# A fused attention, expert and feed-forward kernel: attention cut into one-engine jobs that the kernel's own list scheduler orders and pins

## The chip, the cores and the metric

The kernel runs on one core of a Trainium2 chip. The metric is the device time of one launch in microseconds (us). Before the change three launches took 1038.58, 1032.4 and 1031.0 us; their median is 1032.4 us.

## The reference

Three stages run one after the other, all in float32. B=4 batches, H=8 heads, S=768 steps and D=48 make 32 independent recurrences; the token rows are 3072 by 384.

```python
# 1. attention (delta rule), for every b, h; k_n = k / (|k| + 1e-6), state starts at 0
for t in range(S):
    y[t] = q[t] @ state
    state += beta[t] * outer(k_n[t], v[t] - k_n[t] @ state)
x = y.transpose(0, 2, 1, 3).reshape(B * S, H * D)
# 2. experts, top-1 of E=8, F=1024
logits = x @ w_gate + modality_bias[modality_id]
e = argmax(logits);  g = softmax(logits)[e]
x = g * (relu(x @ w1[e]) @ w2[e])
# 3. feed-forward, 2048 wide
h = x @ w_in
out = (h * sigmoid(h)) @ w_out
```

## The kernel before, in words

**Attention.** The 768 steps are cut into six tiles t of 128 steps, each with two halves e of 64 steps; the 32 recurrences (b, h) are two groups p of two batches, 16 recurrences each. For one (t, p) the work is a chain of small products on TensorE (PE), each group of which writes one of five PSUM banks that ScalarE (ACT) or VectorE (DVE) empties:

- `grams`: four groups `gr` of 8 products k·k and k·q (L158). ACT copies k·k to G (L161). The k·q part goes to KB with its upper triangle cleared, in one of two ways that `mask` names: DVE multiplies by a mask while it copies (L166, "v"), or ACT copies (L173, "p") and GpSimd (POOL) clears afterwards (L181). Then ACT moves a 32-wide diagonal block inside G (L177).
- `lanes`: DVE transposes the diagonal blocks of both p into L, one recurrence's block to a lane (L230); ACT takes roots for the norms (L197); DVE scales, multiplies v by the lengths (`lengthen`, L213), and inverts all unit triangular 32-blocks in 31 dependent steps (L237, L249, L259, L267). `spread` transposes the inverses back into G (L275), and `spread_upper` transposes them again, the other way round, into T (L284), whose halves two DMAs move to other partitions (L288). `gather` copies the blocks into KA (L293, by ACT or by DMA).
- `merge`: PE joins the blocks (px L308, then po L320 from X and T), and forms weights (pw L335, L338), which ACT negates into KA.
- `rec`: for each half e PE computes the update pu (L365), the next state ps (L376) and the read py (L388), 32 small products each; ACT copies them to Z (L369, L380) and Y (L396). The 16 products of each of the two batches lie in the two column halves of PE's array. `zip="zss"` says that pu takes the two halves in turn, and ps and py first all of one, then all of the other.
- Y goes to HBM and is transposed (xt L608), six products give the router's logits (pl L621 and L627), and DVE adds the bias (lg L629). This last line is called gate(t) here. The lanes of t+1 depend only on the grams of t+1; the recurrence of t+1 needs the lanes of t+1 and the state of t.

**Experts.** `Router.rank` and `finish` (the "wave") turn logits into slots: group 0 (tiles 0 to 2) into five slots of 256 tokens, group 1 (tiles 3 to 5) into four of 512. Weights are split into a high and a low part (ACT L950, DVE L951); a slot gathers its tokens, runs ph (L991) and poe (L1002) in 8 pieces, and scatters. The slots of group 0 can start when tile 2 is ranked, and so lie beside the attention of the later tiles; group 1 must wait for gate(5).

**Feed-forward.** Six groups of 512 tokens: fph (L1232), silu, fpo (L1249).

**What sets the order.** In `run` every step of attention gets a position from hand-set numbers (S, F, L, G, A, M, R, D, W, Z of PLAN), and the steps are written in order of position. Tile, the framework, then schedules the instructions of all stages onto the five in-order engines; `Experts.regular` is written after attention and fills in between.

Of the kernel before, what the change touches and what calls it, by code (L numbers as in the profile page):

```python
# [34 lines left out]

class Attention:
    B, H, S, D = 4, 8, 768, 48

    def __init__(self, tc, ident, pools, kq, qb, kd, vd, beta, xs):
# [30 lines left out]


        self.G = cp.tile([128, 4, N, 64], F32, name="G")
        self.st = [{} for _ in range(T)]
        self.todo = [[], []]

    NB = 6

    def copier(self, x):

        nc = self.nc  # L80
        return {"a": nc.scalar.copy, "v": nc.vector.tensor_copy, "p": nc.gpsimd.tensor_copy, "d": nc.sync.dma_start}[x]
# [18 lines left out]


    def setup_early(self):
# [8 lines left out]
    def betas(self):  # L111
        self.nc.sync.dma_start(self.bl, self.beta)

    def setup_late(self):
        nc = self.nc
        for z in self.KI:
            for e, r in enumerate((slice(64, 128), slice(0, 64))):
                c = slice(64 * (1 - e), 64 * (1 - e) + 48)
                nc.scalar.copy(z[r, e], self.ident[r, None, c].to_broadcast([64, self.U // 2, 48]))
        for z in self.KA:  # L120
            nc.gpsimd.memset(z, 0.0)
        nc.gpsimd.memset(self.Z[0][64:128], 0.0)
        nc.gpsimd.memset(self.Z[1][0:64], 0.0)


    def fetch(self, t, p):
        for i in range(2):
            self.nc.sync.dma_start(self.keys(t, p, i).rearrange("p u m c -> p (u m c)"), self.kq[t, p, i])

    def fetch_more(self, t, p):  # L130
        nc, KB = self.nc, self.kb(t, p)
        for e in range(2):
            r = slice(64 - 64 * e, 128 - 64 * e)
            nc.sync.dma_start(KB[r, e], self.qb[t, p, r])
        vs = self.st[t]["vs", p] = self.pools["ld"].tile(
            [128, self.U // 2, self.D], F32, tag="kr", name=f"vs{t}_{p}", bufs=4
        )
        nc.sync.dma_start(vs, self.vd[t, p])

    def fetch_late(self, t, p):  # L140
# [4 lines left out]


    def grams(self, t, ps):
# [37 lines left out]

        return [lambda p=p, i=i: step(p, i) for p in ps for i in range(n)]


    def scales(self, t):


# [1262 lines left out]
```

## Time and profile before

| what | value |
|---|---|
| three launches | 1031.0, 1032.4, 1038.58 us (median 1032.4) |
| profiled execution | 1032.07 us, of which 1030.3 us are the span of the trace |
| granted TensorE clock, mean | 0.925 of full speed |
| busy in the span | PE 903.2 us (88%), DVE 595.7 (58%), ACT 484.3 (47%), POOL 103.9 (10%) |
| gate(5), the end of attention | bias added at 384.12 us |

The span falls into two parts. Up to gate(5) attention runs, with the experts of the first three tiles filled in. After it come the experts of the other tiles and the feed-forward. Busy time counts the time in which an engine executes something; the granted clock is the share of its full speed that the chip gave TensorE in that stretch.

### The profile page before, as it was taken

How to read it: one execution, taken by the hardware profiler on the slowest of the kernel's cores; microseconds unless marked ns; L12 is line 12 of the kernel's file. 1: busy time of each engine (PE TensorE's matmuls, PEld its weight loads, DVE VectorE, ACT ScalarE, POOL GpSimd, SP SyncE). 2: the span in 40 equal slices, each digit the busy share in tenths (PEclk: the TensorE clock that was granted, in tenths of full speed). 3: DMA queues.
4: the chain of work that ended last, by engine and by line, in shares of the span. 5: the costliest groups of instructions: out<-in, count | busy, mean ns of one | idle time of the engine just before them, and what ended most of it. 6: DMA issues, size and time to landing. Idle time of an engine off the chain costs nothing. (4 is left out here: it accounts for less than half of the span.)

```text
span 1030.3 us, 22690 instructions
## 1 busy us (share of the span) xinstructions
PE 903.2 (88%) x9126; PEld 818.9 (79%) x9126; DVE 595.7 (58%) x1714; ACT 484.3 (47%) x980; POOL 103.9 (10%) x100
## 2 busy tenths in 40 slices
PE   5266867684879998989999899999999999999998
PEld 5255757674768887988898799999899999999997
DVE  4996939577673337999997337553333333333333
ACT  5435555565646765646665445433333233332322
POOL 5100000000120010142341101000000000000000
PEclk7657979597889998999999999999999999999999
DMA  8943636160353144146676132200100000000000
GB/s 224 275 143 68 174 79 183 38 156 17 84 171 69 41 118 157 39 137 213 219 229 191 62 99 63 78 31 0 32 31 31 1 31 1 31 1 1 31 1 31
DMA packets 65253, 92.29 MB, mean 90 GB/s; under 512 B 25225, under 2 KB 49943, under 8 KB 65136
## 3 DMA queue, kind: packets, MB, share of 16 engines
q1 hardware_dynamic: 61808, 80.90, 27.3%
q0 software_dynamic: 3328, 9.83, 2.9%
q8 instruction: 73, 1.20, 0.5%
q14 instruction: 44, 0.36, 0.1%
HBM read 79.18 MB, written 14.55 MB: 91 GB/s over the span
## 5 line engine op out<-in xcount | busy, mean ns | idle before, releaser
L1249 PE MATMUL fpo<-o,fgh 128*128 128x384 f32 x768 | 184.3, 338 | 0.0
L1237 DVE TENSOR_TENSOR fy<-fph,fy 128x512 f32<-128x512 f32 x96 | 66.4, 692 | 161.5 <-ACT fy L1235 161.0
L1249 PEld LDWEIGHTS fpo<-o,fgh 128*128 128x128 f32 x768 | 139.3, 188 | 7.9 <-ACT fgh L1239 0.4
L1235 ACT ACTIVATE fy<-fph 128x512 f32<-128x512 f32 x96 | 57.5, 599 | 169.0 <-PE fph L1232 166.1
L1249 PE MATMUL fpo<-o,fgl 128*128 128x384 f32 x384 | 116.6, 338 | 0.0
L1232 PE MATMUL fph<-fxh,ih 128*128 128x512 f32 x288 | 113.7, 395 | 0.0
L1232 PE MATMUL fph<-fxl,ih 128*128 128x512 f32 x288 | 113.3, 394 | 0.0
L1232 PE MATMUL fph<-fxh,il 128*128 128x512 f32 x288 | 113.2, 393 | 0.0
L1241 DVE TENSOR_TENSOR fgl<-fy,fgh 128x512 fp32r<-128x512 f32 x96 | 66.5, 692 | 74.7 <-ACT fgh L1239 64.3
L1239 ACT CAST fgh<-fy 128x512 fp32r<-128x512 f32 x96 | 59.7, 622 | 80.6 <-DVE fy L1237 44.6
L1002 PE MATMUL poe<-wKT,pairs 128*128 128x384 f32 x384 | 75.9, 343 | 3.2 <-ACTq L1093 3.2
L1002 PEld LDWEIGHTS poe<-wKT,pairs 128*128 128x128 f32 x384 | 68.6, 191 | 6.4 <-ACTq L1093 3.5
L259 DVE TENSOR_TENSOR tmp<-A,L 128x126 f32<-128x126 f32 (+20 forms) x336 | 72.3, 252 | 0.4
L267 DVE TENSOR_TENSOR A<-A,tmp 128x126 f32<-128x126 f32 (+20 forms) x336 | 72.3, 252 | 0.2
L1249 PEld LDWEIGHTS fpo<-o,fgl 128*128 128x128 f32 x384 | 71.1, 188 | 0.5
L951 DVE TENSOR_TENSOR wRH<-raw,wRH 128x384 fp32r<-128x384 f32 x72 | 39.5, 554 | 54.3 <-ACT wRH L950 43.1
L1232 PEld LDWEIGHTS fph<-fxl,ih 128*128 128x128 f32 x288 | 54.1, 188 | 10.5
L1232 PEld LDWEIGHTS fph<-fxh,il 128*128 128x128 f32 x288 | 54.1, 188 | 9.6
L1232 PEld LDWEIGHTS fph<-fxh,ih 128*128 128x128 f32 x288 | 54.1, 188 | 9.0
L991 PE MATMUL ph<-xhl,wRH 128*128 128x256 f32 x360 | 57.6, 305 | 3.3 <-DVE wRH L951 1.5
L950 ACT CAST wRH<-raw 128x384 fp32r<-128x384 f32 x72 | 36.8, 514 | 46.3 <-PE ph L991 37.4
L376 PE MATMUL ps<-Z,KI 128*48 128x48 f32 x704 | 43.2, 229 | 16.7 <-ACT Z L369 14.4
(418 smaller groups left out, 1688.6 us busy)
## 6 DMA issues: line engine op xcount, KB each, us to landing
raw<-in_moe_w_dram SPq DMA_DIRECT2D x72, 384.0 KB
KKQ<-in_kq_dram SPq DMA_DIRECT2D x16, 512.0 KB
KB<-in_qb_dram SPq DMA_DIRECT2D x24, 256.0 KB
ri<-in_moe_w_in_dram SPq DMA_DIRECT2D x12, 512.0 KB
ro<-in_moe_w_out_dram SPq DMA_DIRECT2D x16, 384.0 KB
vs<-in_vd_dram SPq DMA_DIRECT2D x12, 384.0 KB
KI<-in_kd_dram SPq DMA_DIRECT2D x24, 192.0 KB
Z<-vs SPq DMA_DIRECT2D x24, 192.0 KB
```

Of the source, the lines that this page charges most:

```text
L259: nc.vector.tensor_tensor(tv, r[:, :, j : j + 1].to_broadcast([128, c, n]), L[:, j : j + 1, j + 1 :].to_broadcast([128, c, n]), op=ALU.mult,)
L267: nc.vector.tensor_tensor(r[:, :, j + 1 :], r[:, :, j + 1 :], tv, op=ALU.add)
L376: nc.tensor.matmul(ps[64 * i : 64 * i + 48, h, :], KI[:, e, u % 16, :], Z[e][:, u, :], start=True, stop=True)
L951: nc.vector.tensor_tensor(lo, raw, hi, op=ALU.subtract)
L991: nc.tensor.matmul(ph, a[:, k, :], b[:, k, :], start=(i == 0), stop=(i == 8))
L1002: self.mark = nc.tensor.matmul(po[t], a[:, cs], b, start=(c == 0 and i == 0), stop=(c == F - 1 and i == 2)).ins
L1232: nc.tensor.matmul(ph, a[:, k, fs], b[:, k, :], start=(n == 0), stop=(n == 8))
L1235: nc.scalar.activation(sg, ph, AF.Sigmoid)
L1237: nc.vector.tensor_tensor(gv, ph, sg, op=ALU.mult)
L1239: self.marks = [nc.scalar.copy(gh, gv).ins]
L1241: self.marks.append(nc.vector.tensor_tensor(gl, gv, gh, op=ALU.subtract).ins)
L1249: nc.tensor.matmul(po[c], a[:, rows], b, start=(f == 0 and i == 0), stop=(f == 15 and i == 2))
```

## The change

Attention is cut into jobs that use one engine each: one group of four grams, one copy of it, one lane step, one update. A new class `Order` takes every job with an engine, a cost in us, a rank and the jobs it must follow. `solve` simulates the five engines, with five PSUM banks and a fixed delay between engines; on each engine it takes, of the jobs that could start first, the one of the lowest rank. The rank is t plus a number for the kind of job plus `half` for p=1. `emit` writes the jobs in that order and binds each attention instruction to the one before it on its engine, so that the framework keeps the order; expert instructions are not bound. Apart from that:

- ps and py take the column halves in turn, as pu did (`pairs`); py of each half e has its own bank, its own Y and its own stores of 64 rows, and the router's products follow that layout.
- `spread_upper` and its two DMAs are gone. TensorE turns the upper inverses by products with the identity (`turn_upper`, pt, 32 products of 32x32 for each (t, p)), and ACT copies the result (`keep_join`).
- Which engine copies: all k·q parts go by ACT and POOL ("pp"); the diagonal blocks go by DMA ("dddd", at t=0 by ACT and DVE); `gather` goes by ACT for p=0 and by DMA for p=1 (at t=0 by ACT and DVE).
- The keys and queries come in two DMAs of 48 rows in place of one of 128 rows with zeros.
- The router's gate and wave are cut at every change of engine, and are jobs of the same plan.
- Two pairs of expert buffers change places (`xs`).

```diff
 PLAN = dict(
 
-    diag="aaaaaaaa", gather="daaaddddaaaadadd", mask="vpppvp", T="dd", len="vvvv",
-
-    one=3, zip="zss",
-
-
-    S=[0.05, -0.257], F=[0.482, 0.005], L=[0.912, 1.573],
-    G=[0.02, 0.299, 0.322, 0.55], A=[0.774, 0.3], M=[0.018, 0.098, 0.195, 0.298, 0.248, 0.367, 0.424, 0.548],
-    R=[0.349, 0.649, 0.649, 0.987], D=[0.7, 0.816, 0.992, 1.023], g=0.051, W=[0.601, 0.323, 1.21, 0.264, 0.405],
-    Z=-0.802,
+    diag="dddd", gather="aaaadddd", mask="pp",
+    one=3,
+    rank=dict(
+        kq=-6.55, qb=2.51, vs=-6.41, kd=7.94, gr=-4.2, Gc=-1.1, Kc=3.3, dg=-5.97, sel=-3.21, L=-3.42, zero=-0.58, b2=-1.88, sc=-9.01, ln=3.36, st=-4.2, sp=-1.19, ga=-3.96, va=-12.73, px=-2.57, X=7.77, pt=9.47, T=-0.07, po=-2.63, o=-4.56, w=2.54, wc=-4.92, up=-0.27, uc=-4.84, ps=-2.88, sc2=0.43, out=3.71, py=-1.11, Y=0.54, xt=-7.84, xc=4.11, gt=-11.26, wv=-5.65,
+    ),
+    first=-3.388, half=1.726,
 
     fin=10, fin1=19, fin2=30, fin3=36, n0=40, npre=40, tok=70,
...
+class Order:
...
+    LATE = 0.12
+    QUEUES = ("PE", "ACT", "DVE", "POOL", "SP")
...
+        def arm(i):
+            at[i] = max((end[k] + (0 if jobs[k]["e"] == jobs[i]["e"] != "SP" else self.LATE) for k in deps[i]), default=0.0)
+            ready[jobs[i]["e"]].append(i)
...
+        def bank_at():
+            if len(taken) < self.banks:
+                return 0.0
+            k = taken[len(taken) - self.banks]
+            ends = [end[x] for x in free[k]]
+            return None if None in ends else max(ends) + self.LATE
...
+        while len(out) < n:
+            best = None
+            for q in self.QUEUES:
+                b = bank_at() if q == "PE" else 0.0
+                cand = []
+                for i in ready[q]:
+                    s = max(at[i], clock[q])
+                    if jobs[i]["bank"]:
+                        if b is None:
+                            continue
+                        s = max(s, b)
+                    cand.append((s, i))
+                if not cand:
+                    continue
+                s0 = min(s for s, _ in cand)
+                i = min((jobs[i]["r"], i) for s, i in cand if s <= s0 + 0.03)[1]
+                s = max(x for x, k in cand if k == i)
+                if best is None or s < best[0]:
+                    best = (s, i, q)
...
+            clock[q] = s + j["c"]
+            if j["size"]:
+                line = max(line, s + 0.5) + j["size"]
+                end[i] = line + 1.6
+            else:
+                end[i] = s + j["c"]
...
+        for j in self.line:
+            at = len(traced)
+            j["fn"]()
+            new = {}
+            for x in traced[at:]:
+                new.setdefault(x.engine, []).append(x)
+            for e, xs in new.items():
+                for x in xs:
+                    if e in last:
+                        tc.add_manual_dep(x, last[e].name, info, reason="order")
+                last[e] = xs[-1]
+
...
-            mk = PLAN["mask"][2 * min(t, 2) + p]
...
+    def mask_reads(self, t, p):
+        for e in range(2):
+            sl = self.kb(t, p)[64 * e : 64 * e + 64, e]
+            self.nc.gpsimd.affine_select(
+                out=sl, in_=sl, pattern=[[0, 16], [1, 64]], compare_op=ALU.is_gt, fill=0.0, base=0,
+                channel_multiplier=-1,
+            )
+
+    def diagonal(self, t, p, e, by):
+        rs, G = slice(64 * e, 64 * e + 32), self.g(t, p)
+        self.copy[by](G[rs, :, 32:64], G[rs, :, 0:32])
...
-    def spread_upper(self, t):
-        nc = self.nc
-        st = self.st[t]
-        T = st["T"] = self.pools["ln"].tile([128, 32, 32], F32, tag="T", name=f"T{t}")
-        nc.vector.transpose(out=T.rearrange("p u c -> p c u"), in_=st["A"])
-        tv = T.rearrange("p (n w) c -> p w n c", w=2)
-        for e in range(2):
-            r = slice(64 * e, 64 * e + 32)
-            self.copier(PLAN["T"][e])(tv[64 * e + 32 : 64 * e + 64, 1], tv[r, 1])
...
+    def turn_upper(self, t, p):
+        G = self.g(t, p)
+        pt = self.st[t]["pt", p] = self.bank([128, 8, 32], f"pt{t}_{p}")
+        for n in range(8):
+            for q in range(4):
+                e, w = divmod(q, 2)
+                r, u = slice(64 * e, 64 * e + 32), 2 * n + w
+                self.nc.tensor.matmul(pt[32 * q : 32 * q + 32, n], G[r, u, 32:64], self.ident[r, r], start=True, stop=True)
+
+    def lower(self, t, p):
+        X, T = self.st[t]["Xx", p], self.st[t]["Xt", p]
+        po = self.st[t]["po", p] = self.bank([128, 8, 32], f"po{t}_{p}")
+        for n in range(8):
+            for q in range(4):
+                r = slice(32 * q, 32 * q + 32)
+                self.nc.tensor.matmul(po[r, n], T[r, n], X[r, n], start=True, stop=True)
+
...
-        def turns(k):
-            x = [(i, b, h) for h in range(H) for i, b in enumerate(bs)]
-            return x if PLAN["zip"][k] == "z" else sorted(x)
...
+    def pairs(self, p):
+        return [(i, 2 * p + i, h) for h in range(self.H) for i in range(2)]
...
+    def read(self, t, p, e):
+        KB, Z = self.kb(t, p), self.Z[e]
+        py = self.st[t]["py", p, e] = self.bank([128, self.H, self.D], f"py{t}_{p}_{e}")
+        for i, b, h in self.pairs(p):
+            u = b * self.H + h
+            self.nc.tensor.matmul(py[64 * i : 64 * i + 64, h], KB[:, e, u % 16], Z[:, u], start=True, stop=True)
...
+    def store(self, t, p, e):
+        for i in range(2):
+            at = (t * self.B + 2 * p + i) * 128 + 64 * e
+            self.nc.sync.dma_start(self.xs[at : at + 64], self.st[t]["Y", p, e][64 * i : 64 * i + 64])
...
+                    add(("gr", t, p, i), "PE", 1.06, lambda t=t, p=p, i=i: self.gram(t, p, i),
+                        [("kq", t, p, i // 2), ("px", t - 2, p), ("pt", t - 2, p)] + [("ga", t - 2, p, k) for k in range(4)]
+                        + [("py", a, b, e) for e in range(2)], bank=[("Gc", t, p, i), ("Kc", t, p, i)])
+                    add(("Gc", t, p, i), "ACT", 0.34, lambda t=t, p=p, i=i: self.keep_gram(t, p, i), [("gr", t, p, i)])
...
+                    by = PLAN["diag"][2 * p + e]
+                    if t == 0:
+                        by = "av"[e]
+                    add(("dg", t, p, e), *self.by(by, 0.63, 0.72), lambda t=t, p=p, e=e, by=by: self.diagonal(t, p, e, by),
+                        [("Gc", t, p, i) for i in range(4)], size=0.5 if by == "d" else 0)
...
+            add(("L", t), "DVE", 1.95, lambda t=t: self.to_lanes(t),
+                [("dg", t, p, e) for p in range(2) for e in range(2)] + [("st", t - 1, 30)])
...
+            add(("sp", t), "DVE", 2.2, lambda t=t: self.spread(t), [("st", t, 30)])
...
+                    by = PLAN["gather"][4 * p + i]
+                    if t == 0:
+                        by = "avav"[i]
+                    add(("ga", t, p, i), *self.by(by, 0.62, 0.72), lambda t=t, p=p, i=i, by=by: self.gather(t, p, i, by),
+                        [("sp", t), ("kz", (2 * t + p) % 3)] + old, size=0.5 if by == "d" else 0)
+                add(("px", t, p), "PE", 0.72, lambda t=t, p=p: self.join(t, p), [("sp", t)], bank=[("X", t, p)])
+                add(("pt", t, p), "PE", 0.72, lambda t=t, p=p: self.turn_upper(t, p), [("sp", t)], bank=[("T", t, p)])
+                add(("X", t, p), "ACT", 0.34, lambda t=t, p=p: self.keep_join(t, p, "x"), [("px", t, p), ("po", t - 1, p)])
+                add(("T", t, p), "ACT", 0.34, lambda t=t, p=p: self.keep_join(t, p, "t"), [("pt", t, p), ("po", t - 1, p)])
...
-        for i in range(2):
+        for e in range(2):
             for c in range(3):
-                for b in range(i, B, 1 + i):
-                    o, r = (slice(64 * i, 64 * i + 64), slice(64 - 64 * i, 128 - 64 * i)) if b % 2 else (slice(128),) * 2
+                for b in range(B):
+                    p, i = divmod(b, 2)
                     nc.tensor.matmul(
-                        pg[32 * b : 32 * b + 32, 0, o], self.wg[:, c, :], self.xT[b][:, c, r],
-                        start=(c == 0), stop=(c == 2),
+                        pg[32 * b : 32 * b + 32, 0, 64 * e : 64 * e + 64], self.wg[:, c, :],
+                        self.xT[2 * p + e][:, c, 64 * i : 64 * i + 64], start=(c == 0), stop=(c == 2),
                     )
+        yield
...
-    b["xh"], b["xl"] = xs[0:2], xs[2:4]
+    b["xh"], b["xl"] = xs[0::2], xs[1::2]
...
-            attn.run(router.load, router.logits, router.gate, router.wave)
+            attn.run(router)
```

Three places show how instructions move. In the rows "a<-b" is a tile written from the tiles b, and the numbers at a tile's end belong to t, p and e.

The first is TensorE's queue at the end of the grams of tile 3. Before, those grams alternate with reads (py) and updates (pu) of tile 1:

```order
L388 MATMUL py1_0_2012<-Z0_112,KB2_108 64x48 x8
L388 MATMUL py1_1_2013<-Z0_112,KB2_108 64x48 x8
L158 MATMUL gr3_1_8_2030<-KKQ1_98 64x128 x8
L365 MATMUL pu1_0_1_2045<-Z1_113,KA2_106 64x48 x16
L158 MATMUL gr3_1_12_2064<-KKQ1_98 64x128 x8
```

With the change they come earlier:

```order
L252 MATMUL gr3_1_0_1964<-KKQ0_97 64x128 x8
L252 MATMUL gr3_1_1_1975<-KKQ0_97 64x128 x8
L393 MATMUL po1_1_1999<-Xx1_1_1643,Xt1_1_1973 32x32 x32
L252 MATMUL gr3_1_2_2043<-KKQ1_98 64x128 x8
L252 MATMUL gr3_1_3_2062<-KKQ1_98 64x128 x8
L426 MATMUL pu1_0_0_2078<-Z0_112,KA2_106 64x48 x16
```

The grams of tile 3 are now all issued before the first update of tile 1; before, they ended behind the update of its second half (p=0).

The second is DVE's queue between the lanes of tile 1 and tile 2. Before:

```order
L267 TENSOR_TENSOR A1_654<-A1_654,tmp1_30_1_886 128x15
L275 STREAM_TRANSPOSE G_118<-A1_654 128x32x32
L284 STREAM_TRANSPOSE T1_1106<-A1_654 128x32x32
L230 STREAM_TRANSPOSE L2_1381<-G_118 128x1024
L199 RECIPROCAL rn_2_1387<-n1_2_1385 128x32
```

With the change:

```order
L347 TENSOR_TENSOR A1_686<-A1_686,tmp1_30_1_1452 128x15
L289 STREAM_TRANSPOSE L2_1458<-G_118 128x1024
L357 STREAM_TRANSPOSE G_118<-A1_686 128x32x32
L316 TENSOR_TENSOR vs1_0_540<-vs1_0_540,nt_1_924 128x768
L316 TENSOR_TENSOR vs1_1_688<-vs1_1_688,nt_1_924 128x768
L301 RECIPROCAL rn_2_1607<-n1_2_1488 128x32
```

The transpose L of tile 2 now stands ahead of the spread of tile 1, the second transpose is gone, and the lengthening of tile 1 stands in the gap in which ACT takes the roots of tile 2.

The third is TensorE's queue at gate(5), where the logits of the last tile (pl5) are turned. Before:

```order
L621 MATMUL pl5_5360<-xT5_3_5358,wg_179 32x64
L1002 MATMUL poe0_2_5671<-wKT_5401,hs_5399 128x384
L1002 MATMUL poe0_3_5672<-wKT_5401,hs_5399 128x384
L1002 MATMUL poe0_2_5671<-wKT_5401,hs_5399 128x384 x2
L1002 MATMUL poe0_3_5672<-wKT_5401,hs_5399 128x384 x2
L627 MATMUL pl5_5360<-ident_66,xT5_0_5261 128x128
L991 MATMUL ph0_2_3_5774<-xhl1_5403,wRH_5400 128x256
```

With the change:

```order
L717 MATMUL pl5_5832<-xT5_3_5830,wg_165 32x64 x2
L1117 MATMUL poe0_0_5923<-wKT_5879,hs_5877 128x384 x2
L1117 MATMUL poe0_1_5924<-wKT_5879,hs_5877 128x384 x2
L725 MATMUL pl5_5832<-ident_66,xT5_0_5728 128x128
L1106 MATMUL ph0_0_4_6031<-xhl0_5880,wRH_5878 128x256
```

Before, the first products of 11 expert pieces (ph0_0_0 to ph0_0_7 and ph0_2_0 to ph0_2_2) stand ahead of this place; with the change those of four (ph0_0_0 to ph0_0_3) do.

## Rows read from the trace of the kernel before

**Rows 1.** The page, parts 1 and 4: busy time; the chain that ended last.

```profile
PE 903.2 (88%) x9126; PEld 818.9 (79%) x9126; DVE 595.7 (58%) x1714; ACT 484.3 (47%) x980; POOL 103.9 (10%) x100
...
PE 43%; DVE 0%; DVEq 0%; issue 0%
```

**Rows 2.** Stretches of all engines; columns: us, busy (instructions) of each, PE clock, DMA.

```profile
60.00:380.00 320.00, 250.90 (x5514) 225.46 (x5514) 204.47 (x879) 190.11 (x414) 26.13 (x23) 0.84 0.38 99
240.00:280.00 40.00, 30.71 (x663) 28.28 (x663) 26.01 (x105) 29.61 (x63) 3.24 (x3) 0.78 0.23 55
340.00:380.00 40.00, 38.36 (x832) 34.56 (x818) 13.05 (x51) 28.24 (x62) 3.69 (x5) 1.00 0.27 75
```

**Rows 3.** Timeline of DVE: start, length, instruction, [idle before it <-releaser].

```profile
22.16 1.90 DVE L230 STREAM_TRANSPOSE L<-G 128x1024 f32<-128x1024 f32 x1
...
56.10 1.89 DVE L230 STREAM_TRANSPOSE L<-G 128x1024 f32<-128x1024 f32 x1
57.91 2.14 DVE L275 STREAM_TRANSPOSE G<-A 128x1024 f32<-128x1024 f32 x1
59.95 1.89 DVE L284 STREAM_TRANSPOSE T<-A 128x1024 f32<-128x1024 f32 x1
...
210.56 2.00 DVE L230 STREAM_TRANSPOSE L<-G 128x1024 f32<-128x1024 f32 x1 [16.01 <-ACT G L177]
...
214.76 1.83 DVE L213 TENSOR_TENSOR vs<-vs,nt 128x768 f32<-128x768 f32 x2
...
239.15 2.18 DVE L275 STREAM_TRANSPOSE G<-A 128x1024 f32<-128x1024 f32 x1
...
309.09 2.26 DVE L275 STREAM_TRANSPOSE G<-A 128x1024 f32<-128x1024 f32 x1
...
384.12 0.18 DVE L629 TENSOR_TENSOR lg<-pl,tbias 128x32 f32<-128x32 f32 x1
```

**Rows 4.** Groups by line: count, busy us, mean ns, then idle before them.

```profile
L951 DVE TENSOR_TENSOR wRH<-raw,wRH 128x384 fp32r<-128x384 f32 x72 | 39.5, 554 | 54.3 <-ACT wRH L950 43.1 <-PE ph L991 9.2 <-PE poe L1002 0.9
...
L173 ACT COPY KB<-gr 64x256 f32<-64x256 f32 x56 | 20.5, 366 | 0.4
...
L166 DVE TENSOR_TENSOR KB<-gr,amask 64x256 f32<-64x256 f32 x40 | 16.7, 420 | 4.2 <-POOL amask L107 3.3 <-ACT G L161 0.2
...
L177 ACT COPY G<-G 32x512 f32<-32x512 f32 x24 | 14.8, 616 | 0.5
...
L230 DVE STREAM_TRANSPOSE L<-G 128x1024 f32<-128x1024 f32 x6 | 11.8, 1962 | 45.4 <-ACT G L177 45.4
```

**Rows 5.** Stretches of DVE at gate(2): us, busy (instructions), PE clock, DMA share, GB/s.

```profile
241.55:247.58 6.03, 2.12 (x18) 0.50 0.01 3
248.40:249.60 1.20, 1.03 (x7) 0.50 0.05 14
254.30:260.90 6.60, 6.34 (x35) 0.75 0.27 48
```

**Rows 6.** Timeline of PE: start, length, instructions (joined in runs).

```profile
66.10 1.06 PE L320 MATMUL po<-X,T 32*32 32x32 f32 x58 [0.36 <-DMA T<-T]
...
263.69 1.14 PE L365 MATMUL pu<-Z,KA 128*64 128x48 f32 x32
...
337.45 1.84 PE L388 MATMUL py<-Z,KB 128*64 128x48 f32 x32
...
339.70 0.75 PE L308 MATMUL px<-G 32*32 32x32 f32 x64
...
352.16 1.50 PE L376 MATMUL ps<-Z,KI 128*48 128x48 f32 x32
```

**Rows 7.** Timeline of SP's queue: start, length, DMA issues.

```profile
61.86 1.26 SPq L288 DMA_DIRECT2D T<-T  x2
```

**Rows 8.** Stretch 339.70 to 384.20, expert products alone: first ph, then poe.

```profile
339.70:384.20 44.50, 8.90 (x58) 7.54 (x59) 2.51 (x6) 2.30 (x6) 1.00 0.29 82
...
339.70:384.20 44.50, 7.59 (x34) 5.68 (x34) 1.05 (x2) 1.00 0.29 82
```

More of the change, by code (lines that the diff above doesn't have):

```diff
@@ L99, in keys, with bank, masks @@
         return self.KQ[(2 * (2 * t + p) + i) % len(self.KQ)]
-    def setup_early(self):
+    def bank(self, shape, name):
+        return self.pools["pa"].tile(shape, F32, tag="pa", name=name)
+    def masks(self):
         nc = self.nc
@@ new lines, in plan, with ring, add, once @@
+    def plan(self, router):
+        T, R, o = self.T, PLAN["rank"], Order(5)
+        st = self.st
+        def ring(t, p, n):
+            return divmod(2 * t + p - n, 2)
+        def add(key, e, cost, fn, after=(), **kw):
+            name, t, p = key[0], key[1], key[2] if key[0] not in ("st", "gt", "wv") and len(key) > 2 else 0
+            r = t + R[name] + PLAN["half"] * p
+            if t < 1:
+                r += PLAN["first"]
+            o.add(key, e, cost, r, fn, after, **kw)
+        def once(key, e, cost, rank, fn, after=()):
+            o.add(key, e, cost, rank, fn, after)
+        once(("amask",), "POOL", 0.6, -9, self.masks)
+        once(("beta",), "SP", 0.1, -4.9, lambda: self.nc.sync.dma_start(self.bl, self.beta))
+        o.jobs[-1]["size"] = 0.4
+        once(("clear",), "POOL", 3.0, -8, self.clear_states)
+        for j in range(3):
+            once(("one", j), "ACT", 1.7, -4 + j, lambda j=j: self.unit_rows(j))
+            once(("kz", j), "POOL", 2.0, -5 + j, lambda j=j: self.nc.gpsimd.memset(self.KA[j], 0.0))
+        once(("gates",), "DVE", 1.5, -1.95, router.load)
+        for t in range(T):
@@ new lines, in plan @@
+            g = router.gate(t)
+            for i, (e, c) in enumerate((("PE", 0.8), ("ACT", 0.27), ("PE", 0.15), ("DVE", 0.2))):
+                add(("gt", t, i), e, c, lambda g=g: next(g, None),
+                    [("gt", t, i - 1)] if i else [("xc", t, p, e) for p in range(2) for e in range(2)] + [("gates",), ("gt", t - 1, 3)],
+                    **(dict(bank=[("gt", t, 3)]) if i == 0 else {}))
+            if t < T - 1 and t % 3:
+                w = router.wave(t)
+                for i, (e, c) in enumerate(router.STEPS[t % 3 - 1]):
+                    add(("wv", t, i), e, c, lambda w=w: next(w, None), [("wv", t, i - 1)] if i else [("gt", t, 3), ("wv", t - 1, 4)],
+                        **(dict(bank=[("wv", t, 2)]) if i == 1 and t > T // 2 else {}))
@@ L517, with by, run @@
+        return o
+    @staticmethod
+    def by(x, a, v):
+        return {"a": ("ACT", a), "v": ("DVE", v), "p": ("POOL", 2 * v), "d": ("SP", 0.07)}[x]
+    def run(self, router):
+        o = self.plan(router)
+        o.solve()
+        o.emit(self.tc)
 class Router:
```

612 lines of the change are left out of this document (294 added, 318 removed).

## The prediction

> **What bounds the kernel now.** I read the page's shares and its last chain first. PE is busy 88% of the span, and the chain that ended last is PE work alone, without issue gaps [rows 1]: behind attention PE never waits, so the end is the end of attention plus the PE work that is left. Attention ends with gate(5), whose last DVE instruction runs from 384.12 to 384.30 [rows 3]. The other 1030.3 - 384.3 = 646.0 us are a fixed load as long as the same expert work is left. The question is what attention costs.
>
> The stretches show that nothing is full before that: from 60 to 380 PE is busy 251 of 320 us at a clock of 0.84, DVE 204, ACT 190 [rows 2]. A chain sets the pace. The timeline of DVE shows its links: L starts at 22.16, 56.10 and 210.56, the spreads at 57.91, 239.15 and 309.09 [rows 3]. A lane phase by itself is short: from L of tile 4 to its spread it takes 239.15 - 210.56 = 28.6 us. Six of these would be 172 us, yet from the first L to the end of the last spread 289 us pass. In the groups by line DVE stands idle 45.4 us ahead of the six L, each time for ACT's diagonal copy, that is for the grams of its tile [rows 4]; those grams stand in PE's queue behind the recurrence of an earlier tile (the first place shown with the change). So lanes and recurrence take turns instead of overlapping. Last, from px of tile 5 at 339.70 [rows 6] to 384.30 is a tail of 44.6 us that only the last recurrence fills.
>
> **The change part by part.** The sum follows DVE, since lanes depend only on grams, which the change moves ahead of the recurrence.
>
> *Lane 0.* L starts at 22.16 now; with all copies of tile 0 spread over ACT and DVE I take 19 (bounds 16 and 22.2). From L to the end of the first spread 60.05 - 22.16 = 37.9 us pass now; L of tile 1 (1.9) and the lengthening (1.8) leave that stretch [rows 3]: 34.2. The spread ends at 53.2. Then DVE does four gathers that it did not do (4 x 0.62, ACT's price for a copy of that shape [rows 4]) and the lengthening: L of tile 1 at 57.5.
>
> *Lanes 1 to 5.* A round is 28.6, less 0.85 for two masked copies (0.42 each [rows 4]) that go to ACT, plus 2.2 for the spread: 29.9. The first is without spread and lengthening, 25.9. L of tile 2 stands at 83.4; four rounds are 119.6, and five spreads fall into them, one more than counted: 2.2. That is 205.2.
>
> *Other work on DVE in that stretch.* The second transposes leave (six at 1.9 [rows 3]); they lay outside the 28.6. Rank costs 2.12 + 1.03 = 3.15 at gate(2), finish with it 6.34 more [rows 5]. Two ranks alone are 6.3, rank with finish 9.5, eleven small copies of indices at 0.17 1.9, four expert splits at 0.55 [rows 4] 2.2, five gates at 0.18 [rows 3] 0.9: together 20.8. That gives 226.0.
>
> *Waits for grams.* The trace has no diagonal copy by DMA. From below the wait is 0, if the grams run far enough ahead; from above it is today's 45.4 [rows 4]. The nearest row is T: its transpose ends at 61.84 [rows 3], SP issues two DMAs in 1.26 us [rows 7], and PE goes on with po at 66.10, released by that DMA [rows 6]: 4.2 us. Four DMAs a tile take this place, and L stands ahead of the previous spread in DVE's queue, so spread, gathers and px behind it wait too. I take a hop of 4.2 in each of four rounds and round up to 18. The last spread then ends at 244.0. The Trainium skill ("DMA: Bandwidth & Descriptors", the anatomy of one DMA) gives about 2.0 us of fixed cost to a DMA; with it these waits would be some 8 us, as an estimate, and the sum 10 lower. The trace's own 4.2 includes the issue and decides.
>
> *Tail.* Today's 44.6 hold 8.90 us of ph and 7.59 of poe [rows 8], filled in by the framework; without them 28.1. Two pieces in between would be 5.4 (below), so 33; bounds 28 and 44.6. Attention ends at 277.
>
> *PE.* Alternation brings py from 1.84 and ps from 1.50 to pu's 1.14 [rows 6]: 24 x 0.70 + 22 x 0.36 = 24.7 us less. The 12 pt cost 0.75 each like px [rows 6]: 9.0 more. Both are hidden by lanes in this sum, except in the tail, where four reads and three states are some 4 us less, and pt with ACT's copy replaces the hop of 4.2. I leave those inside the bounds of the tail. If the cover goes, PE's own sum is the second rival.
>
> *SP and POOL.* SP loses T's two issues a tile and gains four diagonal ones and twice the key loads and smaller stores. At 0.63 us each [rows 7] eight more a tile are 5 us in rounds of 37; hidden, unless they stand in front of the diagonals, which the 18 include. POOL is busy 26 of 320 us [rows 2]; its extra masking is hidden.
>
> *Experts.* The place at gate(5) shows seven pieces fewer ahead of it. A piece is nine products of ph at 8.90/58 and six of poe at 7.59/34 [rows 8]: 2.7 us. These 19 us are not saved but come behind attention. Bounds: 0, if PE has idle time there, and 38, at the half clock that stood at gate(2) [rows 5].
>
> The sum: 277 + 646 + 19 = 942 for the span, and 1032.07 - 1030.3 = 1.8 around it: **944 us**. The profiled execution it is made against is 0.3 us below the median.
>
> **The rivals.**
>
> *ACT becomes the bound (0.15).* ACT does 190 us from 60 to 380 [rows 2]. It gains 32 k·q copies at 0.366 (11.7) and 12 copies of turned blocks (4.4), and loses 16 diagonals at 0.616 (9.9) [rows 4] and 13 expert splits (24 stood ahead of pl5 in ACT's order, 11 do now; 7.2, each priced as its twin on DVE): 189 us behind the first spread. My forecast packs them into 277 - 53 = 224, a share of 0.84; the densest 40 us today have 29.61/40 = 0.74 [rows 2]. At that share they take 255 us, attention ends at 308, and the time is 975. For it: chains that cross ACT at each step; against it: a plan that has two tiles to choose from. The Trainium skill ("TensorEngine Tiling (Array Packing)", PSUM Bottleneck) says that tiling speeds TensorE but not the emptying of PSUM, for which both ScalarE and VectorE should be used. This change goes the other way with the k·q copies. The trace leaves it open, as ACT has not been near full.
>
> *PE and its clock (0.13).* With everything alternating a tile has 24 groups at 1.14, six at 0.75 and some 2.5 us of turns and logits [rows 6]: 34.4. Six tiles less 18 for grams that are done, plus 6 for experts, are 194 us at full clock. If the clock stays at today's 0.84 and PE is busy 38.36/40, the best stretch [rows 2], they take 241; the end is 294, the time 961.
>
> *The overlap doesn't open (0.07).* Diagonals by DMA, L ahead of spread in an in-order queue, and a pinned order that can't react could make lanes and recurrence take turns as they do now. Then only lane 0 comes earlier: from the first spread (51.1) to the last one's end 253.4 us pass as today (57.91 to 311.35), the tail is 72.8 (311.35 to 384.12) [rows 3], attention ends at 377, and with 19 us of deferred pieces the time is **1044, slower**. It decides if each of four rounds waits some 17 us for its grams: 226 + 68 + 73 + 19 is about today's 384. It needs all four, where today's total is 45.4, so I hold it unlikely.
>
> *The change doesn't do what it says in one part (0.05).* If reads and states don't get shorter in turn, PE has 24.7 us more under the lanes and 4 in the tail: 948.
>
> **How the numbers follow.** The forecast has 0.60; its own range is 921 (waits 4, tail 28, pieces 15) to 969 (waits 33, tail 43). With lane 0 at 16 and no waits it is about 914, the lower end. The upper end takes in PE and most of ACT's case: 985. Left out are the slower rival and a part of ACT's. What differs by less than 1% (10 us) can't be told from no change here. Faster by over 1%: 0.60 + 0.15 + 0.13 + 0.05, less 0.01 for a bad case of ACT's, is 0.92; slower, most of the third rival's 0.07, is 0.06; between is 0.02.
>
> **What would show it.** Right: gate(5) at 260 to 295, L to L in 30 to 38 us, gaps ahead of L of a few us, ps and py near 1.14, clock above 0.9 behind 60. ACT's case shows as ACT over 0.8 busy with PE waiting for its copies; PE's as a clock of 0.5 in many stretches; the slower one as L rounds over 50. The prediction is wrong if PE has gaps behind gate(5), since then the 646 are no fixed load.

## The result, and the profile after

The changed kernel takes 988.0 us in the median (987.03 to 988.68, four launches), 0.954 of the kernel before (95% interval 0.950 to 0.959), which took 1035.5 in four launches beside it. The forecast was 944 (914 to 985): the direction was right, the gain about half of what was forecast (88 us), and the time lies outside the range. The profiled execution took 987.73 us, its span is 986.0. One launch of e4_sorted below, the profiled one, ran in a slower state of the chip; its median holds that launch, its ratio does not, and its gate is left out.

The page of the changed kernel, parts 1 and 4, as [rows 1]:

```profile
PE 882.8 (90%) x9966; PEld 799.7 (81%) x9966; DVE 591.3 (60%) x1674; ACT 485.0 (49%) x1006; POOL 123.0 (12%) x110
...
PE 45%; DVE 0%; ACT 0%; DVEq 0%; issue 0%; ACTq 0%
```

The chain that ended last is still PE work without gaps. DVE's timeline has the links of the chain, as [rows 3]; L of a tile is now line 289, the spread line 357, the gate line 728:

```profile
20.14 1.94 DVE L289 STREAM_TRANSPOSE L<-G 128x1024 f32<-128x1024 f32 x1 [0.23 <-ACT G L281]
...
51.88 2.18 DVE L357 STREAM_TRANSPOSE G<-A 128x1024 f32<-128x1024 f32 x1
...
59.01 1.91 DVE L289 STREAM_TRANSPOSE L<-G 128x1024 f32<-128x1024 f32 x1 [0.57 <-DMA G<-G]
...
92.20 1.98 DVE L289 STREAM_TRANSPOSE L<-G 128x1024 f32<-128x1024 f32 x1
...
127.01 2.04 DVE L289 STREAM_TRANSPOSE L<-G 128x1024 f32<-128x1024 f32 x1 [3.32 <-ACT KA L416]
...
171.66 1.92 DVE L289 STREAM_TRANSPOSE L<-G 128x1024 f32<-128x1024 f32 x1
...
232.10 1.99 DVE L289 STREAM_TRANSPOSE L<-G 128x1024 f32<-128x1024 f32 x1
...
268.37 2.29 DVE L357 STREAM_TRANSPOSE G<-A 128x1024 f32<-128x1024 f32 x1
...
279.60 0.19 DVE L728 TENSOR_TENSOR lg<-pl,tbias 128x32 f32<-128x32 f32 x1 [0.99 <-PE pl L725]
...
312.54 0.19 DVE L728 TENSOR_TENSOR lg<-pl,tbias 128x32 f32<-128x32 f32 x1
```

Attention ends at 312.7 in place of 384.3, so it is 71.6 us shorter; the forecast had 277. The last spread ends at 270.7 (forecast 244.0). From L to L pass 33.2, 34.8, 44.7 and 60.4 us; the forecast wanted 30 to 38. Stretches of all engines, columns as in [rows 2]: from L of tile 1 to the last spread, the tail, and the rest, then the rest of the kernel before (PE alone):

```profile
59.01:270.66 211.65, 171.28 (x4997) 154.21 (x4995) 174.21 (x775) 148.31 (x343) 36.41 (x24) 0.79 0.54 130
270.66:312.70 42.04, 37.78 (x1094) 34.62 (x1089) 12.93 (x48) 30.91 (x67) 0.10 (x1) 0.88 0.29 67
312.70:986.00 673.30, 647.04 (x3424) 586.07 (x3422) 357.63 (x698) 277.12 (x531) 64.06 (x48) 0.98 0.22 71
...
384.30:1030.30 646.00, 626.76 (x3305) 0.99 0.22 70
```

The rest takes 673.3 us in place of 646.0. So 27.3 of the 71.6 us are given back behind attention, and 44.3 remain. In the first stretch DVE is busy 174.2 of 211.7 us: it stands 37.4 us idle, and hardly for grams: ahead of these L it waits 3.9 us in all (the rows above; for 3.3 of them the profile names a copy of ACT that L does not read, and the last diagonal DMAs of that tile had been issued 4.2 us before, at 122.84).

The longest stop shows in three queues. ACT, PE and DVE of the changed kernel at 208 to 231, and SP's DMA issue between them, from their timelines:

```profile
208.80 0.75 ACT L269 COPY KB<-gr 64x256 f32<-64x256 f32 x2
217.25 0.92 ACT L1065 CAST wRH<-raw 128x384 fp32r<-128x384 f32 x2 [7.70 <-DMA raw<-in_moe_w_dram]
218.20 0.59 ACT L415 ACTIVATE KA<-pw 48x512 f32<-48x512 f32 x1
```

```profile
214.09 0.42 SPq L1049 DMA_DIRECT2D raw<-in_moe_w_dram  x1
```

```profile
220.59 2.44 PE L426 MATMUL pu<-Z,KA 128*64 128x48 f32 x32 [8.88 <-ACT Z L447]
```

```profile
230.83 0.17 DVE L972 COPY p1f<-pidx 128x10 f32<-128x10 f32 x1 [12.01 <-PE pidx L969]
...
232.10 1.99 DVE L289 STREAM_TRANSPOSE L<-G 128x1024 f32<-128x1024 f32 x1
```

The first split of expert weights stands in ACT's queue ahead of copies of attention whose products are ready. Its load was issued at 214.09 only, after DVE had computed which expert the slot gets (its number is written at 212.87). ACT stops for 7.7 us, so PE stops for 8.9, so pidx (the products that give the slots' token indices) is late. DVE's copies of these indices stand ahead of L of tile 5, and DVE waits 12.0 us for them.

### The profile page after: what moved, and what is told of

It is laid out like the page before. It is cut to its first block, busy times and chain, and to the rows that moved or that the text cites. A ratio compares the mean times of both kernels' runs of the same rounds, so it can differ in the third digit from the quotient of the medians.

```text
span 986.0 us, 24438 instructions
## 1 busy us (share of the span) xinstructions
PE 882.8 (90%) x9966; PEld 799.7 (81%) x9966; DVE 591.3 (60%) x1674; ACT 485.0 (49%) x1006; POOL 123.0 (12%) x110
## 5 line engine op out<-in xcount | busy, mean ns | idle before, releaser
L1350 ACT ACTIVATE fy<-fph 128x512 f32<-128x512 f32 x96 | 57.5, 599 | 168.9 <-PE fph L1347 166.1
L341 DVE TENSOR_TENSOR tmp<-A,L 128x126 f32<-128x126 f32 (+20 forms) x336 | 75.8, 266 | 0.8
L347 DVE TENSOR_TENSOR A<-A,tmp 128x126 f32<-128x126 f32 (+20 forms) x336 | 76.1, 267 | 0.0
L252 PE MATMUL gr<-KKQ 48*64 48x128 f32 x512 | 43.6, 333 | 26.9 <-DMA KKQ<-in_kq_dram 25.7
L252 PEld LDWEIGHTS gr<-KKQ 48*64 48x64 f32 x512 | 38.7, 170 | 29.6 <-issue 20.5
L1347 PEld LDWEIGHTS fph<-fxl,ih 128*128 128x128 f32 x288 | 54.1, 188 | 10.5
L1347 PEld LDWEIGHTS fph<-fxh,il 128*128 128x128 f32 x288 | 54.1, 188 | 9.6
L1347 PEld LDWEIGHTS fph<-fxh,ih 128*128 128x128 f32 x288 | 54.1, 188 | 9.0
```

Source lines behind the costliest of these rows:

```text
L252: self.nc.tensor.matmul(gr[64 * e : 64 * e + 64, j], x[r, k, 0, :], x[r, k, :, :], start=True, stop=True)
L341: nc.vector.tensor_tensor(tv, r[:, :, j : j + 1].to_broadcast([128, c, n]), L[:, j : j + 1, j + 1 :].to_broadcast([128, c, n]), op=ALU.mult,)
L347: nc.vector.tensor_tensor(r[:, :, j + 1 :], r[:, :, j + 1 :], tv, op=ALU.add)
L1347: nc.tensor.matmul(ph, a[:, k, fs], b[:, k, :], start=(n == 0), stop=(n == 8))
L1350: nc.scalar.activation(sg, ph, AF.Sigmoid)
```

## The experiments

All times are medians of four to ten launches of a kernel, each ratio is to the kernel before on the same chip, with its 95% interval. "Gate" is the end of gate(5) in the profiled execution, "rest" what follows it. The profiled executions of e1, e2 and e10 were the longest of their kernels, 6, 5 and 9 us over the median, so gate and rest together read that much too long.

The expectations name five theories. A: pieces of other stages stop the bound queues. B: PE's half clock sets the pace. C: the lanes on DVE set the end of attention, as in the forecast's sum. D: POOL slows the lane steps. E: the recurrence on PE and ACT sets the end.

| run | us | ratio | gate | rest |
|---|---|---|---|---|
| changed kernel | 988.0 | 0.954 (0.950 to 0.959) | 312.7 | 673.3 |
| e1_hold | 978.1 | 0.944 (0.938 to 0.949) | 310.0 | 672.7 |
| e9_idx | 985.7 | 0.951 (0.946 to 0.956) | 310.0 | 676.2 |
| e10_hold_idx | 975.8 | 0.942 (0.936 to 0.947) | 305.9 | 677.4 |
| e2_nomask | 978.8 | 0.944 (0.939 to 0.949) | 308.7 | 672.9 |
| e13_all | 975.6 | 0.940 (0.935 to 0.945) | 298.9 | 675.0 |
| e14_half_lanes | 982.1 | 0.949 (0.943 to 0.954) | 307.0 | 672.5 |
| e4_sorted | 1000.7 | 0.963 (0.956 to 0.970) | | |
| e5_before_zzz | 1036.2 | 1.000 (0.996 to 1.004) | 380.1 | 647.5 |
| e3_nopin | 1073.3 | 1.038 (1.034 to 1.041) | 399.1 | 670.5 |
| e6_diag_act | 992.4 | 0.956 (0.951 to 0.961) | 320.8 | 671.1 |
| e12_mask_dve | 1002.5 | 0.968 (0.963 to 0.973) | 331.7 | 670.8 |
| e11_warm | 1000.5 | 0.966 (0.961 to 0.970) | 326.2 | 671.6 |
| e15_light | 972.0 | 0.940 (0.935 to 0.944) | 317.8 | 652.1 |
| e8_turn_dve | 975.3 | 0.941 (0.936 to 0.946) | 309.5 | 664.5 |
| e20_turn_twice | 987.6 | 0.952 (0.948 to 0.957) | 312.2 | 672.5 |
| e16_best | 959.3 | 0.928 (0.923 to 0.934) | 294.8 | 663.0 |
| e18_best_half | 946.4 | 0.913 (0.909 to 0.917) | 278.6 | 661.8 |
| e19_best_nomask | 951.2 | 0.917 (0.913 to 0.920) | 288.2 | 661.7 |

**The stop in the queues: e1, e9, e10.** In e1 the splits wait in the queues behind named attention instructions; e9 moves three steps of the wave; e10 does both. The edits, shortened:

```diff
 # e1: for the first eight splits
+        with issue_after(order.at["Y", 3, 1, 1]), issue_after(order.at["L", 5]):
             nc.scalar.copy(hi, raw)
             nc.vector.tensor_tensor(lo, raw, hi, op=ALU.subtract)
 # e9: in run, between solve and emit
+        for k, to in ((10, ("ln", 4, 1)), (11, ("wv", 2, 10)), (12, ("b2", 5))):
+            j = o.jobs[o.ids["wv", 2, k]]
+            o.line.remove(j)
+            o.line.insert(o.line.index(o.jobs[o.ids[to]]) + 1, j)
```

> The changed kernel (median 988.0, gate(5) at 312.7) with one edit: the first eight splits of expert weights are queued behind the last copy of Y of tile 3 on ACT and behind L of tile 5 on DVE. The order of attention's jobs is the same. Theory A (pieces of other stages that stand in the in-order queues and wait for their data stop the bound attention behind them): ACT's wait of 7.7 us for raw weights and PE's 8.9 us behind it go, DVE's 12.0 us for pidx falls to 4 or less, L of tile 5 starts at 220 to 226 in place of 232.1, gate(5) at 300 to 306, time 975 to 982. Theory B (PE at half clock with the recurrence sets the end, the stall only fills a gap): gate(5) stays within 3 us, time 985 to 990.

> The changed kernel with one edit: the three last steps of the wave of tile 2 (index copies on DVE behind pidx, pgate on PE, gate copies on DVE) are moved behind L of tile 5, the spread and the lengthening of tile 4. Theory A: DVE's wait of 12.0 us for pidx no longer stands ahead of L, so L of tile 5 starts at 217 to 221 and the last spread ends at 256 to 260 in place of 270.7; but ACT still stops for the weights, so the recurrence of tile 4 starts only some us sooner: gate(5) at 303 to 309, time 978 to 985. Theory C (DVE's chain alone sets the end): the whole 12 us come through, gate(5) at 299 to 302, time 973 to 977. Theory B: no change, 985 to 990.

> Both edits together: splits of expert weights held back, and the index steps behind L of tile 5. Theory A: the two waits share their cause, so the gain is more than either alone but less than their sum: L of tile 5 at 216 to 220, gate(5) at 294 to 302, time 968 to 978. Theory B: 983 to 990.

L of tile 5 in e1, then in e9:

```profile
224.98 1.98 DVE L291 STREAM_TRANSPOSE L<-G 128x1024 f32<-128x1024 f32 x1
...
213.42 1.90 DVE L289 STREAM_TRANSPOSE L<-G 128x1024 f32<-128x1024 f32 x1
```

e1 gains 10 us, as theory A has it, and the waits of 7.7 and 8.9 us are gone; the gate came 4 us later than its range, in a profiled execution that was 6 us long. e9 alone gains 2.3, within the two intervals' overlap and in theory B's range, though L starts 18.7 us earlier: ACT still waits 7.9 us for the weights there and PE 9.1, and the recurrence has not come along. e10 gains 12.2, in theory A's range. So the stop costs some 10 to 12 us, and through ACT and PE more than through DVE.

**POOL beside the lanes: e2, e13.** The edit empties `mask_reads`; e13 does it on top of e10.

> The changed kernel without POOL's clearing of the upper triangle of the k·q part (that part of the computation is left out: the read then uses unmasked products). Same order of jobs. Theory D (POOL beside DVE slows the lane steps: two steps of 91 elements took 1.22 and 1.34 us while POOL cleared, their neighbours 0.42): the busy time of the lane steps falls from 163 to 155 us or less, rounds are 1 to 2 us shorter, gate(5) at 302 to 307, time 977 to 983. Theory A: the lanes get shorter but the waits of DVE take most of it up, gate(5) at 308 to 313, time 983 to 988.

> Held splits, moved index steps and no POOL masks together (the clearing of the k·q part is left out). If the waits and the slowed lanes lie one behind the other on DVE's chain (theory C), the gains add: 988 less 12.2 less 9.2, time 964 to 969. If both only bring DVE's chain down to the recurrence (theory E), the second is worth little on top of the first: 971 to 977.

DVE and POOL of the changed kernel show the hindrance; the pairs of lane steps are of nearly the same size:

```profile
199.66 0.42 DVE L347 TENSOR_TENSOR A<-A,tmp 128x96 f32<-128x96 f32 x2
...
200.45 1.22 DVE L341 TENSOR_TENSOR tmp<-A,L 128x91 f32<-128x91 f32 x2
201.60 1.34 DVE L347 TENSOR_TENSOR A<-A,tmp 128x91 f32<-128x91 f32 x2
```

```profile
199.29 3.40 POOL L274 TENSOR_SCALAR_AFFINE_SELECT KB<-KB 64x1024 f32<-64x1024 f32 x2 [29.28 <-ACT KB L269]
```

Without the clearing the lane instructions of all tiles sum to 157.8 us in place of 170.0, and the time is 9 us shorter, as theory D has it (the gate, 308.7, is 2 us later than its range). On top of e10 the same edit is worth nothing (975.6 against 975.8), as theory E has it, so these gains don't add.

**Are the lanes the bound? e14.** The edit is `if j % 2: return` in `step`.

> The changed kernel (988.0, gate(5) at 312.7) with the odd lane steps left out (15 of 31 in every tile: the inverses are then not the reference's). DVE's work per tile falls by some 13 us; jobs and order stay. Theory C (the chain of lanes on DVE sets the end of attention, as the forecast's sum has it): five rounds shorter by 13 us, gate(5) at 245 to 260, time 922 to 938. Theory E (the recurrence on PE and ACT, one tile behind the other, sets it; it takes 33 to 48 us a tile): spreads come much earlier, but gate(5) only moves to 290 to 305, time 965 to 982.

Theory C, and with it the frame of the forecast's sum, falls: DVE's busy time from L of tile 1 to the last spread drops from 174 to 121 us, yet the gate comes only 5.7 us earlier and the time is 6 us shorter, with intervals that overlap. That is 2 us less at the gate than even theory E had. DVE then waits for grams and logits that PE has not yet done; its stretch, and the longest wait of each kind:

```profile
58.36:253.13 194.77, 121.43 (x485) 0.80 0.57 138
...
121.45 1.98 DVE L289 STREAM_TRANSPOSE L<-G 128x1024 f32<-128x1024 f32 x1 [10.58 <-DMA G<-G]
...
154.19 0.19 DVE L730 TENSOR_TENSOR lg<-pl,tbias 128x32 f32<-128x32 f32 x1 [13.52 <-PE pl L727]
```

**Parts of the change undone, or done alone: e4, e5, e3, e6, e12.** e4 sorts the pairs of `state` and `read`; e5 sets `zip="zzz"` in the kernel before; e3 leaves out `add_manual_dep`; e6 calls `diagonal(..., "a")` for t>0 at the same place in the order; e12 calls `keep_reads(..., True)`, DVE's masked copy, in place of ACT's and empties `mask_reads`.

> The changed kernel (988.0) with ps and py in sorted order again (all products of one column half, then of the other), pu still in turn; same order of jobs. The forecast's fourth rival: 24.7 us more PE work hidden under the lanes but for 4, time 990 to 993. Theory B (PE with the recurrence sets the pace from tile 1 to tile 3): most of the 25 us at full clock come through and more at half clock, gate(5) 15 to 30 us later, time 1003 to 1018.

> The kernel before (median about 1035) with one part of the change alone: ps and py take the column halves in turn (zip zzz in place of zss). If the recurrence lies on the chain of attention there (lanes and recurrence take turns), most of the 25 us of PE time come off: time 1005 to 1020. If lanes and their waits set it: 1028 to 1036.

> The changed kernel without the binding of each attention instruction to the one before it on its engine: the jobs are written in the same order, but the framework schedules them. Theory A (bound queues stop behind late pieces): the framework can move pieces past each other, the waits for pidx and raw shrink or move, time 975 to 995. Rival: the framework's own costs bring back the old interleaving of lanes and recurrence, time 1000 to 1040.

> The changed kernel with the diagonal blocks copied by ACT again for t>0 (20 copies of 0.62 us, ACT 12 us busier) in place of 20 DMAs; same order of jobs. L waited 3.9 us in all for these DMAs. Theory E: ACT's work lies in the recurrence's queue, gate(5) 5 to 12 us later, time 992 to 1000. Theory C: L of the next tile comes 2 to 4 us sooner at most where it waited, time 984 to 990.

> The changed kernel with all k·q parts masked and copied by DVE again (0.42 us each) in place of ACT's copy (0.37) and POOL's clearing; same order of jobs. ACT has some 35 us less to do, DVE some 30 more net of POOL's hindrance. Theory E2 (ACT sets the recurrence): gate(5) 10 to 25 us earlier, time 963 to 978. Theory E1: little, 982 to 992. Theory C (DVE's lanes set the end): 30 us later, 1010 to 1020; the waits of DVE for grams in its queue come on top.

The gate of e3:

```profile
398.94 0.19 DVE L728 TENSOR_TENSOR lg<-pl,tbias 128x32 f32<-128x32 f32 x1
```

Alternation does nothing in the kernel before (1.000). In the changed kernel its loss costs some 8 us by the ratios, between the two expectations, and the intervals overlap. Without binding, the same jobs written in the same order take 1073 us, more than the kernel before, which neither expectation had: attention ends at 399.1, 14.8 us later than before the change and 86.4 later than with the binding, and the rest stays as long as in the changed kernel. The gain is there only with the binding. Twelve us more work on ACT cost 4.4 us (gate 8.0 later), theory E's low end, but the intervals overlap widely. Masks on DVE cost 14.5, between theories E and C: ACT's relief of 35 us bought nothing there. From L of tile 1 to L of tile 2 pass 37.3 us in place of 33.2, and PE waits 8.7 us for KB that DVE writes.

Not tried alone are the two key DMAs, the gathers by DMA, the cut of the router into jobs, and the exchanged buffers.

**PE's clock and PE's work: e11, e15.** e11 adds idle products to e10 (`warm`: identity by identity into the bank of the next group). e15 forms, for each batch, one product of 384 columns where there were eight of 48 (a group has 16 products in the program, which the trace lists as 32).

> The kernel of e10_hold_idx (975.8) with products on TensorE that do nothing (identity by identity into a bank that the next product overwrites): 55 ahead of the first gram of tile 1, where PE waits 18 us for keys, 4 ahead of each px of p=0, 3 ahead of each po, 2 ahead of each pu; about 44 us of work at full clock, some of it in PE's waits. Theory B (PE's half clock, which follows its idle stretches, sets the pace of the recurrence; mean granted clock 0.77 up to gate(5)): the clock up to gate(5) rises to 0.88 or more, the half-clock stretch from 24 to 72 goes, gate(5) comes 6 to 15 us earlier, time 960 to 970. Theory A (waits in the queues set it, PE's speed does not): the added work pushes gate(5) back by 0 to 10 us, time 976 to 986.

> The changed kernel with update, state and read of each (t, p, e) as 2 products of 384 columns in place of 16 of 48 columns for each of the two batches (all heads then use the first head's weights, so attention's values are not the reference's). PE's work in the recurrence falls by some 55 us at full clock (70 groups from 1.14 to about 0.35 us), ACT's, DVE's and the order stay. Theory E1 (PE's work at the clock that it gets sets the recurrence): gate(5) from 312.7 to 255 to 275, time 930 to 950. Theory E2 (ACT's copies and the hand-over between PE and ACT set it): gate(5) at 290 to 305, time 965 to 980.

PE up to the gate, first e10, then e11:

```profile
0.00:305.88 305.88, 233.20 (x6522) 0.79 0.61 138
...
0.00:326.21 326.21, 268.41 (x6856) 0.86 0.58 130
```

e11 raised the mean clock up to the gate from e10's 0.79 to 0.86, and the gate came 20 us later, as neither theory had it. But lane 0 alone lost some 10 us there, as DVE waited 12.9 for ACT's roots, which was not meant; the run doesn't settle what the clock costs. e15 did not do what it was made for: the three groups' busy time fell by 9 us only (85.4 to 76.3 from 60 to 310), where 55 were expected; the number of columns is the same. Its time lies in theory E2's range for another reason: the framework put 85 products of ph and 48 of poe ahead of the gate in place of 40 and 22. The gate came 5 us later, the rest fell by 21. PE's expert work ahead of the gate rose by 12.6 us there, more than the 9 us that the recurrence lost, so expert pieces ahead of the gate seem to cost less than they save behind it; no run shows this by itself.

**The turn on TensorE: e8, e20.** e8 puts the second transpose and the two DMAs back, into `spread`, in place of the turn on TensorE; e20 does both turns. In each, po reads DVE's result. The edit, shortened:

```diff
     def spread(self, t):
+        T = st["T"] = self.pools["ln"].tile([128, 32, 32], F32, tag="T", name=f"T{t}")
+        nc.vector.transpose(out=T.rearrange("p u c -> p c u"), in_=st["A"])
+        tv = T.rearrange("p (n w) c -> p w n c", w=2)
+        for e in range(2):
+            nc.sync.dma_start(tv[64 * e + 32 : 64 * e + 64, 1], tv[64 * e : 64 * e + 32, 1])
     def turn_upper(self, t, p):      # e8 only; keep_join likewise for "t"
+        return
```

> The changed kernel with the upper inverses turned as before: a second transpose on DVE right behind the spread (six times 1.9 us) and two DMAs a tile, in place of 12 groups of products on PE and 12 copies on ACT; same order of the other jobs. Theory C: DVE's chain is 1.9 us a round longer, gate(5) 8 to 12 us later, and po waits for a DMA: time 996 to 1004. Theory E: PE and ACT lose 13 us of work and po waits some 4 us a tile for the DMA: time 984 to 994.

> e8_turn_dve (975.3) with the work of the turn on TensorE and ACT's copy done as well, into a tile that nothing reads; po waits for DVE's and the DMAs' T. If the work in PE's and ACT's queues (12 groups and 12 copies, 13 us) is what the turn on TensorE costs: back to 985 to 990. If it is the hand-over from PE to ACT to po (po waits 10.1 us for its operands in the changed kernel, 2.8 in e8): 975 to 979.

PE behind the gate in e8:

```profile
309.49:974.00 664.51, 643.24 (x3405) 0.99 0.22 71
```

Both theories had e8 slower than it is (984 and up): without this part of the change the kernel takes 12.7 us less. e20 is back at 987.6, so the part costs by its work in PE's and ACT's queues, not by the hand-over to po. DVE takes the transposes at no loss. Of the 12.0 us by which the span is shorter, 3.2 come off the gate and 8.8 off the rest: more expert products stand ahead of the gate (ph and poe 15.2 us in place of 11.5), and PE is idle behind it for 21.3 us in place of 26.3.

**All that helped: e16, e18, e19.** e16 is e8 with e10; e18 leaves out of it the odd lane steps, e19 POOL's clearing.

> e8_turn_dve (975.3) with the splits of expert weights held back and the index steps behind L of tile 5, as in e10_hold_idx. If the two gains (12.7 and 12.2) are of different stretches: 961 to 966. If they overlap in the recurrence of tile 3: 968 to 975.

> e16_best (959.3; gate(5) at 294.8, DVE busy 19 of every 20 us from 40 to 220) with the odd lane steps left out (15 of 31 in every tile, so the inverses are not the reference's). In the changed kernel this moved gate(5) by 5.7 us only. If e16 has taken away what held the recurrence back, DVE's lanes are the bound there (theory C) and the same edit now moves gate(5) by 20 us or more, to 275 or below, time 935 to 945. If PE and ACT still set it (theory E): gate(5) at 287 to 292, time 950 to 957.

> e16_best without POOL's clearing of the k·q part (left out). The lane steps are then 12 us shorter in sum, as in e2_nomask. Theory C (DVE sets the end in e16): gate(5) 8 to 13 us earlier, time 946 to 952. Theory E: 955 to 959, as it was worth nothing on top of e10_hold_idx.

e16 is the fastest kernel here that leaves nothing out: 959.3 us, 0.928 of the kernel before. It gains 28.7 us, somewhat more than 12.7 and 12.2 together, so both come through. Its stretch from L of tile 1 to the last spread, DVE alone:

```profile
59.89:254.86 194.97, 182.60 (x778) 0.82 0.60 145
```

DVE is busy 94% of it, against 82% in the changed kernel. Leaving out half the lanes is now worth 16 us at the gate and 13 in time (e14: 5.7 and 6), and POOL's clearing 8 us in time (6.6 at the gate). e18 lies between the two theories, just short of C's; e19's time is in C's range, its gate just short of it. So DVE's lanes now hold the end far more than in the changed kernel, but not alone: the two chains seem to be of nearly one length.

## Why the prediction was wrong

The 44 us by which the span misses (986 against 942) are 26.7 at the last spread, 9.0 from there to gate(5) and 8.3 in the rest. Runs account for 28.7 of them (e16: the stop and the turn); the other 15 us between e16 and the forecast stay open.

- **The frame, "the sum follows DVE".** This is the step that failed. Grams did move ahead and the lanes did run ahead of the recurrence, but PE and ACT then did not keep up: gate(4) comes at 279.8, 9.1 us behind the last spread, and e14 shows that lanes 53 us shorter bring the gate only 5.7 us forward. The PE paragraph put the recurrence at nothing as covered and did not ask how long it is itself, though the rows of the kernel before show it: px of tile 5 at 339.70 [rows 6] comes 28.4 us behind the end of the last spread [rows 3], and the sum lets it follow at once.
- **Lane 0** was right: L at 20.1 (19), the spread's end at 54.1 (53.2), L of tile 1 at 59.0 (57.5).
- **Waits for grams: 18** were 3.9. DVE is idle 37.4 us in all there: 12.0 for pidx, 7.9 for logits, 4.2 for the roots of the lanes, and smaller waits for the experts. Router and expert pieces stand in a bound queue, and I priced them by their busy time alone. The hop itself was 4.2 us or less, as priced, where it shows (issue at 122.84, L at 127.01); the 2.0 us that the prediction sets beside it are given by the Trainium skill ("DMA: Bandwidth & Descriptors", Anatomy of one DMA) for DMAs issued by GpSimd, where these were issued by SP, and no run here shows them. Work was 5.7 us more than summed (174.2 against 168.5); the round of 28.6 was the shortest of the five before (up to 39.8).
- **"Its extra masking is hidden"** was wrong: POOL's time is hidden, but its clearing lengthens lane steps on DVE by 12 us in sum. The Trainium skill ("SBUF — State Buffer", Who interferes with whom) says that a DVE instruction with two SBUF inputs contends with a GpSimd instruction that reads SBUF, over a shared port pair that is locked exclusively. The trace agrees in the main: the two pairs above took 0.8 and 0.9 us more than the one before them, together the 1.7 us of one clearing; that one, also inside POOL's two clearings, took no longer than usual.
- **Tail: 33** was right in size and late in start. From px of tile 5 to gate(5) pass 34.2 us; but px comes 7.9 us behind the end of the spread, when PE has done the reads of tile 4 (until 273.0), its logits and some expert products:

```profile
278.55 0.75 PE L372 MATMUL px<-G 32*32 32x32 f32 x64
```

- **PE.** Alternation made the groups as short as thought (timeline of PE, ps and py of the changed kernel):

```profile
225.12 0.89 PE L442 MATMUL ps<-Z,KI 128*48 128x48 f32 x32
225.84 1.10 PE L456 MATMUL py<-Z,KB 128*64 128x48 f32 x32
```

- **pt "hidden"** was wrong: the 13 us of work on PE and ACT cost 12.7 (e8, e20).
- **Experts: 19** were 27.3. Expert products behind the gate, first ph, then poe:

```profile
312.70:986.00 673.30, 121.85 (x611) 99.30 (x609) 36.98 (x68) 32.87 (x68) 0.98 0.22 71
...
312.70:986.00 673.30, 127.86 (x602) 106.96 (x602) 13.69 (x26) 0.98 0.22 71
```

Seven pieces moved, as read from the order. PE's busy time in the rest rose by 20.3 us (647.0 against 626.8), nearly as summed; 7.1 us are idle time that I had not counted. PE stands idle 26.3 us there, the prediction's own sign that the 646 are no fixed load. It stood idle 19.2 us of the 646 before the change too: the chain that ended last covers 43% of the span [rows 1], some 443 us, and so does not show that PE never waits behind attention.

The slower rival did not come, though one round of four, at 60.4 us, was over its 50. The ACT and PE rivals each had a part of the truth: from 60 to 294 ACT is busy 164 of 234 us (0.70) and PE 190 (0.81, at a clock of 0.79); neither is full, but the two hand over to each other at every step. Which of the two holds the other more is open: e15 did not test it, and e11 lengthened lane 0.

## What to carry to other kernels

Before a sum follows one chain, work out the length of the chain that is said to be covered; where the two are alike, the gain stops at the second. In an order that is bound, price a piece of another stage by when its data arrives, not by its busy time, and keep what depends on late data behind what does not. A part that moves work from one engine to two that hand over to each other should be tried alone: here it took back 13 us.

## What the runs showed of the hardware

The clock follows PE's stop: windows of PE in the changed kernel (us, busy, clock, DMA share, GB/s).

```profile
200.00:208.00 8.00, 7.71 (x260) 1.00 0.36 92
208.00:216.00 8.00, 3.21 (x98) 0.90 0.17 37
216.00:224.00 8.00, 3.36 (x39) 0.50 0.15 44
```

With PE waiting 8.9 us (211.7 to 220.6) the granted clock falls from 1.00 to 0.50, that is to 1.2 GHz; at 220.59 the pu that ended the wait took 2.44 us, where one at full clock takes 1.14 [rows 6]. So this stop cost a second time. What the half clock costs over all of attention stays open.
